# A new opening for a fused state-space and MLP kernel: loads, decay differences and weight decoding in another order

## The chip, the cores and the metric

The kernel runs on one core of a Trainium2 chip. The time is the device time of one execution in microseconds (us). Of the kernel before, three executions were timed: 346.02 us is the median, 344.71 and 346.83 the ends. One more execution was profiled; it took 345.45 us, and the profile's rows are from it. The engines are named as the profile has them: PE (TensorE, matmuls), DVE (VectorE), ACT (ScalarE), POOL (GpSimd) and SP, whose queue issues most transfers. Each engine works through its own instructions in order and waits for others by semaphores.

## What is computed

Two blocks follow each other. The first is a chunked state-space scan (4 batches, 8 heads, 768 positions, head dimension 32, state size 16):

```python
cum = np.cumsum(np.log(a_chunk), axis=-1)
L = np.exp(cum[:, :, :, None] - cum[:, :, None, :]) * causal
M = np.einsum('bhin,bhjn->bhij', Cc, Bc) * L
y = M @ xc + np.einsum('bhin,bhnd->bhid', Cc, state) * np.exp(cum)[..., None]
state = decay_full * state + np.sum(Bx * decay_from_j, axis=2)
```

The second is an MLP on the 3072 tokens of 256 channels that come out of it: `h = x @ w_in` (256x2048), `g = h * clip(h + 3, 0, 6) / 6`, `out = g @ w_out` (2048x256). The weights arrive as float64.

## The kernel before

The 768 positions are cut into six chunks of 128 (c = 0 to 5). A chunk holds the tokens of all four batches (512 columns) and is treated as two halves of 64 positions. Chunk c goes through the scan while TensorE works on the MLP of chunk k = c - 1; only chunk 0 has its scan ahead of everything. The order of all instructions is written out by hand: the calls in the source are the program, and on each engine the instructions stand in the order of the calls. No planner moves them.

**The scan of a chunk.** L, the decay factors, is the exponential of differences of `cum`. For chunks 0 and 1 the differences are made on TensorE: `in_three` splits `cum` into three bf16 parts (`split`), then into a PSUM bank for each batch go a mask (`diff_mask`, L352), a product that subtracts the column's value (`diff_less`, L364) and 16 small products that add the row's (`diff_pick`, L373); `diff_exp` (L381, ACT) takes the exponential. `turn_b` and `turn_squares` turn B and C. `ends` (L412, POOL) scales B by the decay to the end of the half. `scores` makes the products of C and B (`cb`, L543) and, through `into_state` (L555), those of B and x for the state of both halves. `multiply` puts L on the scores in four products on DVE (L585), one for each pair of heads; `mid` (L580) is the state between the halves. `mix` (L611) multiplies with x, for heads 0 to 3 (`ys[..., 0]`) and then 4 to 7, and adds what comes from `mid` (`from_state`, L516). `keep` (L625) copies chunk 0's result to `yT`, and `renew` makes the state for the next chunk.

**The weights.** w_in and w_out arrive in eight blocks of 1 MB (`raw`, three buffers): blocks 0 to 3 are w_in, each four of the 16 column groups f; blocks 4 to 7 are w_out. `decode` takes the 64-bit floats apart and makes float32: exponent and sign on ACT and DVE, the significand on DVE (L209, L213), the sign put back by L236, and a last product (L249) that writes `first_in[i]` or a quarter of `w_out`. It is a generator of five steps; `weights(i, n)` takes n of them. Its fourth step also issues the load of block i + 3 (`load_w`).

**The first MLP pass** (k = 0) is float32. For each f, `mlp_in` makes two products of 512 columns (L636, each issued as two matmuls); `ramp` (L715, ACT) and `times_ramp` (L720, DVE) make g in `gT`. PSUM has four banks for it (`f0` to `f3`, f modulo 4). Between the groups stand the steps of blocks 2 to 5, laid out by the table `weave`: block i has its five steps after f = 4i - 8 to 4i - 4. Then `first_out` (L735) multiplies with w_out, in four quarters that need blocks 4 to 7 in turn, with the scan of chunk 1 and the split of w_in into fp32r parts between them. The later passes use those parts (`lead`, `follow`, L684) and `wide_units` (L861), with the next chunk's scan in fixed places.

**The opening's queues.** On SP: `a`, C in eight pieces, x, block 1, the stores of `cum`, blocks 2 and 3. On ACT's queue: block 0, then B. `busy` is a product whose result nobody reads, called twice.

## Time and profile before

| what | us |
|---|---|
| median of three executions | 346.02 |
| the profiled execution | 345.45 |
| its span, first to last instruction | 343.7 |
| PE busy in the span | 334.6 (97%) |
| DVE / ACT / POOL busy | 220.1 / 173.2 / 142.7 |
| first matmul of the first MLP pass issued | 22.98 |
| first matmul with w_out issued | 50.55 |

A row of the timeline gives the start in us from the start of the span, the duration (of a merged group: from its first start to its last end), the engine, the line, the operation, what it writes and reads, shape and type, and how many were merged; in brackets the idle time of the engine just before and what ended it. Instructions of one engine overlap a little, so the next can start before the last one's duration is over. "PE" rows are matmuls, "PEld" rows the weight loads beside them. `raw` stands in the profile for the weight blocks, `wse` and `wm` for their parts, `w` for the decoded blocks.

### The profile page before, as it was taken

The numbers are of one execution on the slowest core, as the hardware profiler recorded it, in microseconds if no ns is written. First come the engines' busy times: TensorE is split into PE (matmuls) and PEld (weight loads), VectorE is DVE, ScalarE is ACT, GpSimd is POOL, SyncE is SP. The second block draws the span as 40 slices with busy tenths as digits, with TensorE's granted clock in tenths as the row PEclk, the third lists the DMA queues.
The fourth block names the chain that finished last, engine by engine and source line by source line (L and its number), as shares of the span: only waits on it lengthen the run. The fifth ranks groups of instructions, "written<-read, shape, count | busy, mean of one in ns | idle before, by whom it ended". The sixth has DMA issues, their size and how long they took to land.

```text
span 343.7 us, 8181 instructions
## 1 busy us (share of the span) xinstructions
PE 334.6 (97%) x3378; PEld 266.5 (78%) x3378; DVE 220.1 (64%) x357; ACT 173.2 (50%) x359; POOL 142.7 (42%) x139
## 2 busy tenths in 40 slices
PE   6889999999999999999999999999999999999996
PEld 2554448888778888888888888888887788888995
DVE  6689999999698647775438666447666324676011
ACT  4769878738874561564551564561564010565000
POOL 3300000093299923099611199610099400089500
PEclk9999999999999999999999999999999999999999
DMA  8888959206941057242029242051200010200010
GB/s 173 163 341 169 242 187 176 53 2 95 192 61 23 5 69 159 34 60 51 2 34 176 46 56 58 6 64 17 34 13 0 2 19 1 34 12 2 0 33 31
DMA packets 91605, 24.89 MB, mean 72 GB/s; under 512 B 84208, under 2 KB 87952, under 8 KB 91056
## 3 DMA queue, kind: packets, MB, share of 16 engines
q1 hardware_dynamic: 87184, 23.06, 34.8%
q10 hardware_dynamic: 4384, 1.31, 1.7%
q8 instruction: 26, 0.43, 0.5%
q14 instruction: 11, 0.09, 0.1%
HBM read 21.07 MB, written 3.29 MB: 71 GB/s over the span
## 4 chain that ended last, share of the span: by engine, by line
PE 75%; issue 11%; DMA 4%; DVE 2%; ACT 2%; POOL 2%; SPq 2%; POOLq 0%; DVEq 0%
PE h L684 31%; PE wb L861 13%; PE wc L861 8%; PE wa L861 8%; PE oa L794 4%; PE ob L794 4%; PE y L611 2%; PE y L516 2%; DMA raw<-in_moe_w_in_dram 2%; PE cb L543 2%; DMA eto<-cum_e 1%; ACT L L401 1%; POOL bs L412 1%; DMA pairs<-in_C_dram 1%; SPq L321 1%
## 5 line engine op out<-in xcount | busy, mean ns | idle before, releaser
L708 DVE SCALAR_TENSOR_TENSOR gT<-gT,h 128x512 f32<-128x512 f32 x80 | 54.9, 687 | 30.7 <-ACT gT L707 27.9
L707 ACT ACTIVATE gT<-h,half_up 128x512 f32<-128x512 f32 x80 | 55.1, 690 | 33.2 <-PE h L684 33.1
L780 POOL TENSOR_TENSOR s<-gT 128x512 f32<-128x512 f32 x20 | 25.8, 1288 | 66.4 <-DVE gT L708 66.4
L684 PE MATMUL h<-gap,w_gap 128*128 128x512 f32 x160 | 51.8, 409 | 0.0
L684 PE MATMUL h<-high,w_high 128*128 128x512 f32 x160 | 50.7, 398 | 0.1
L684 PE MATMUL h<-low,w_low 128*128 128x512 f32 x160 | 50.3, 395 | 0.0
L700 ACT ACTIVATE h<-h 128x512 f32<-128x512 f32 x40 | 23.5, 588 | 30.4 <-PE h L684 30.4
L684 PEld LDWEIGHTS h<-high,w_high 128*128 128x128 f32 x160 | 29.5, 188 | 8.5 <-DVE h L697 2.1
L684 PEld LDWEIGHTS h<-low,w_low 128*128 128x128 f32 x160 | 30.1, 188 | 7.2
L684 PEld LDWEIGHTS h<-gap,w_gap 128*128 128x128 f32 x160 | 29.9, 188 | 7.1 <-DVE gap L678 0.5
L401 ACT ACTIVATE L<-L,cum_n 128x64 f32<-128x64 f32 x128 | 31.6, 337 | 0.7 <-POOL L L162 0.7
L861 PE MATMUL wb<-s,w_out 128*128 128x256 f32 x128 | 30.7, 382 | 0.0
L419 POOL TENSOR_TENSOR tmp<-state,eto 128x256 f32<-128x256 f32 x5 | 3.6, 721 | 61.0 <-ACT eto L405 60.9
L735 PE MATMUL o<-w_out,gT 128*128 128x256 f32 x128 | 28.7, 381 | 0.0
L697 DVE TENSOR_SCALAR h<-h 128x512 f32<-128x512 f32 x40 | 27.7, 692 | 1.2 <-PE h L684 1.2
L636 PE MATMUL h<-yT,w 128*128 128x512 f32 x64 | 27.7, 594 | 0.0
L780 POOL TENSOR_TENSOR s<-s,gT 128x512 f32<-128x512 f32 x20 | 26.9, 1345 | 1.6
L585 DVE TENSOR_TENSOR L<-L,cb 128x512 f32<-128x512 f32 x24 | 15.3, 682 | 19.1 <-PE cb L543 16.3
L735 PEld LDWEIGHTS o<-w_out,gT 128*128 128x128 f32 x128 | 24.1, 190 | 3.8 <-issue 0.5
L861 PEld LDWEIGHTS wb<-s,w_out 128*128 128x128 f32 x128 | 24.0, 190 | 3.6
L412 POOL TENSOR_TENSOR bs<-B,L 128x128 f32<-128x128 f32 x24 | 13.7, 584 | 30.9 <-ACT L L401 25.8
L780 POOL TENSOR_TENSOR gT<-gT 128x512 f32<-128x512 f32 x20 | 25.9, 1294 | 0.0
(141 smaller groups left out, 534.3 us busy)
## 6 DMA issues: line engine op xcount, KB each, us to landing
raw<-in_moe_w_out_dram SPq DMA_DIRECT2D x4, 1024.0 KB
L<-cum_d SPq DMA_DIRECT2D x8, 512.0 KB
xt<-in_x_dram SPq DMA_DIRECT2D x6, 512.0 KB
raw<-in_moe_w_in_dram SPq DMA_DIRECT2D x3, 1024.0 KB
out_dram<-back SPq DMA_DIRECT2D x128, 16.0 KB
eto<-cum_e SPq DMA_DIRECT2D x20, 64.0 KB
B<-in_B_dram SPq DMA_DIRECT2D x5, 256.0 KB
raw<-in_moe_w_in_dram ACTq DMA_DIRECT2D x1, 1024.0 KB
```

Source lines behind the costliest of these rows:

```text
L401: nc.scalar.activation(Ls[c][:, b, h], Ls[c][:, b, h], AF.Exp, bias=cum_n[:, c, g:g + 1])
L412: nc.gpsimd.tensor_tensor(out=bss[c][:, hs], in0=Bs[c][:, hs], in1=Ls[c][:, b, :, HT - 1:HT].to_broadcast([P, NH, N]), op=ALU.mult)
L636: nc.tensor.matmul(out=h.rearrange("p r i -> p (r i)"), lhsT=first_in[f // FP][:, j, f % FP * P:(f % FP + 1) * P], rhs=yTs[k][:, j], start ...
L684: nc.tensor.matmul(out=h, lhsT=w[:, j, f * P:(f + 1) * P], rhs=y[:, j], start=(start and j == 0), stop=True, skip_group_check=True)
L697: nc.vector.tensor_scalar(out=h, in0=h, scalar1=-Z / UP, scalar2=None, op0=ALU.mult)
L700: nc.scalar.mul(h, h, -Z / UP)
L707: nc.scalar.activation(g, h, AF.Relu, bias=half_up, scale=UP * UP / 6.0)
L708: nc.vector.scalar_tensor_tensor(out=g, in0=g, scalar=UP, in1=h, op0=ALU.min, op1=ALU.mult)
L735: nc.tensor.matmul(out=o[:, b % 2], lhsT=gTs[0][:, f, b * P:(b + 1) * P], rhs=w_out[:, f], start=(f == 0 and b % 2 == 0), stop=True, skip_ ...
L780: nc.gpsimd.tensor_tensor(out=o, in0=p_, in1=q_, op=op)
L794: nc.tensor.matmul(out=bank[:, slot], lhsT=lhs[:, j], rhs=rhs[:, j], start=(clear and j == 0), stop=True, skip_group_check=True)
L861: nc.tensor.matmul(out=bank[:, slot], lhsT=lhs[:, j], rhs=rhs[:, j], start=(clear and j == 0), stop=True, skip_group_check=True)
```

## The change

- **Loads.** C of chunk 0 now comes in one transfer with tokens first, on ACT's queue; B follows `a` on SP. Block 0 is loaded in two halves of 512 KB. The first follows B, the second and blocks 1 and 2 are held: `hold` writes one word of the buffer on GpSimd, with an operand that some earlier step produces, and the load has to wait for that write. The second half waits for the first step of `fade_end`, block 1 for the end of `multiply(0)`, block 2 for the second half of `yT`.
- **Decay differences.** `spread_heads` writes `split` eight times over, once for each head with all other heads zeroed: for chunk 0 half on DVE and half on ACT, for chunk 1 on POOL. `diff_rows` then adds the row's value with two products of 512 columns for each batch in place of `diff_pick`'s 16. Chunk 1's batch 3 is done after f = 1 of the first MLP pass; its exponentials after f = 4, 5, 7.
- **C of chunk 0** is turned on TensorE (`turn_c`, bank `y1`); `fade_end` makes the faded second half on POOL out of the two parts.
- **State.** For chunk 0, `into_state` is called for each half by itself: the first half's after the scores, the second's behind the mixing; `take` and `renew(0)` come later, the latter after f = 13.
- **Decoding.** The exponent comes from `Abs` on ACT; the two `and` steps on DVE go, and the sign is put back by one SCALAR_TENSOR_TENSOR, in blocks 6 and 7 by a product with `Sign` from ACT. Blocks 0 and 1 are decoded in halves (`decode_half`): block 0 around the mixing, block 1 after f = 1 and 2. `weave` starts three groups later, and `by_token` moves to ACT. Both calls of `busy` go.
- **Later chunks.** `apart`, with which the two halves of a mix are issued in different units, holds for chunk 4 too.

```diff
-        Bs[c] = tokens_first(B, nc.scalar if c == 0 else nc.sync, name="B")
-        if c == 0:
-            bcs[c] = [pairs_first(C), Bs[c]]
-        elif c < TURN:
+        if c < TURN:
+            bcs[c] = [tokens_first(C, nc.sync if c else nc.scalar, name="C", tag="bc")]
+        Bs[c] = tokens_first(B, name="B")
...
+    def hold(t, after):
+
+        nc.gpsimd.tensor_copy(t.bitcast(FP32), after)
...
+        signed = i >= NP + 2
+        nc.scalar.activation(e.bitcast(BF16), top.bitcast(BF16), AF.Abs)
...
-        nc.vector.tensor_scalar(
-            out=e, in0=s, scalar1=0x7FF0, scalar2=None, op0=ALU.bitwise_and)
-        nc.vector.tensor_scalar(
-            out=s, in0=s, scalar1=0x8000, scalar2=None, op0=ALU.bitwise_and)
...
+        if signed:
+            nc.vector.tensor_tensor(out=e, in0=e, in1=s, op=ALU.mult)
+        else:
+            nc.vector.scalar_tensor_tensor(
+                out=e.bitcast(U16), in0=top, scalar=0x8000, in1=e.bitcast(U16),
+                op0=ALU.bitwise_and, op1=ALU.bitwise_or)
+        if i + NRAW < 2 * NP:
+            load_w(i + NRAW)
+        yield
         nc.vector.scalar_tensor_tensor(
             out=dst, in0=m, scalar=unit, in1=e, op0=ALU.mult, op1=ALU.mult)
...
+    def diff_rows(c, b):
+        for a, rows in enumerate(HALF):
+            nc.tensor.matmul(
+                out=ds[c, b][rows], lhsT=by_batch[:, b:b + 1].to_broadcast([P, HT]),
+                rhs=spread[c][:, :, rows], start=False, stop=True,
+                tile_position=(0, a * HT), skip_group_check=True)
...
+    for b in range(3):
+        mask(0, b)
+    spread_heads(0, nc.vector, range(NH // 2))
+    spread_heads(0, nc.scalar, range(NH // 2, NH))
+    spread_heads(1, nc.gpsimd, range(NH))
+    add_up(ends_at[1])
+    for b in range(NB):
+        diff_less(0, b)
+    for b in range(2):
+        diff_rows(0, b)
+    turn_c(0, turn_ps(0, 0))
+    for b in range(2, NB):
+        diff_rows(0, b)
     for b in range(NB):
         diff_exp(0, b)
+    turn_b(0)
     first_eto()
...
+    part_early(0)
+    halves = [decode_half(0, u) for u in range(2)]
+    next(halves[0])
+    next(halves[0])
+    fading = fade_end(0)
+    load_half(1, next(fading)[0:1, 0, 0:1])
+    next(fading)
     scores(0)
+    for b in range(2):
+        diff_less(1, b)
+    for b in range(2):
+        diff_rows(1, b)
+    into_state(0, 0)
     multiply(0)
+    load_w(1, Ls[0][0:1, 0, NH - 1, 0:1])
+    next(halves[0])
+    yTs[0] = y_tile("yT", FP32)
+    mix(0, (0,))
+    keep(0, 0)
+    mix(0, (1,))
+    into_state(0, 1)
+    keep(0, 1)
+    c_ps = ps.tile([P, NC, G], FP32, name="c_ps", tag="f3")
+    turn_cum(c_ps)
+    take(0)
+    load_w(2, yTs[0][0:1, 1, 0:1])
+    for _ in range(3):
+        next(halves[1])
+    by_token(c_ps)
     load_w(3)
...
     for i in range(2, NP + 2):
         for j in range(5):
-            weave.setdefault(4 * i - 8 + j, []).append(i)
-    weave[NF - 1].append(NP + 2)
+            weave.setdefault(4 * i - 5 + j, []).append(i)
...
                 for i in weave.get(f, []):
                     weights(i, 1)
-                if f in (6, 8):
-                    diff_exp(c, f // 2 - 3)
+                if f in (1, 2):
+                    for _ in range(3):
+                        next(halves[f - 1])
+                if f == 1:
+                    diff_mask(c, 3)
+                    diff_less(c, 3)
+                    diff_rows(c, 3)
+                elif f == 2:
+                    load_w(1 + NRAW)
+                elif f == 13:
+                    renew(0)
+                if f in (4, 5, 7):
+                    diff_exp(c, {4: 3, 5: 0, 7: 1}[f])
...
-                apart = c in (TURN, NC - 1)
+                apart = c >= TURN
```

## The prediction

> **What bounds the kernel now.** I read the profile's slices first. TensorE (PE) is in the nines from the third slice of 8.6 us to the end, VectorE (DVE) only until about 86 us.

> ```profile
> ## 2 busy tenths in 40 slices
> PE   6889999999999999999999999999999999999996
> ...
> DVE  6689999999698647775438666447666324676011
> ```

> Then the table by stretches, cut where the stages change (columns: stretch, its length, each engine's busy time, clock, DMA). The first product of the first MLP pass is issued at 22.98 and the first product with w_out at 50.55.

> ```profile
> 0.00:23.00 23.00, 17.38 (x451) 10.07 (x451) 17.12 (x37) 12.75 (x22) 5.80 (x18) 1.00 0.90 226
> 23.00:50.50 27.50, 27.50 (x66) 12.24 (x65) 24.92 (x39) 23.40 (x30) 0.00 (x0) 1.00 0.84 195
> 50.50:66.00 15.50, 15.50 (x73) 13.61 (x72) 15.12 (x21) 12.20 (x12) 0.00 (x0) 1.00 0.86 153
> 66.00:85.00 19.00, 18.95 (x391) 15.94 (x389) 17.47 (x25) 11.61 (x36) 12.52 (x12) 1.00 0.26 42
> ```

> From 23 us on, TensorE never waits (27.50 of 27.50, 15.50 of 15.50; the table of waits for it is empty from 50 us to the end). So the time is the moment when the first MLP product starts, plus TensorE's work, plus every wait put into that work. VectorE is nearly as full: 24.92 of 27.50, since between the ramps of the first pass it also decodes the weights. The third view is the timeline of VectorE in that pass:

> ```profile
> 34.06 1.23 DVE L249 SCALAR_TENSOR_TENSOR w<-wm,wse 128x1024 f32<-128x1024 f32 x1
> 35.21 0.68 DVE L720 SCALAR_TENSOR_TENSOR gT<-gT,h 128x512 f32<-128x512 f32 x1
> ...
> 37.20 0.68 DVE L720 SCALAR_TENSOR_TENSOR gT<-gT,h 128x512 f32<-128x512 f32 x1
> 38.50 0.69 DVE L720 SCALAR_TENSOR_TENSOR gT<-gT,h 128x512 f32<-128x512 f32 x1 [0.62 <-ACT gT L715]
> 39.11 1.22 DVE L213 SCALAR_TENSOR_TENSOR wm<-raw,wm 128x1024 f32<-128x1024 uint32 x1
> 40.25 0.68 DVE L720 SCALAR_TENSOR_TENSOR gT<-gT,h 128x512 f32<-128x512 f32 x1
> 40.84 0.68 DVE L236 TENSOR_TENSOR wse<-wse 128x1024 uint16<-128x1024 uint16 x1
> 41.56 1.23 DVE L249 SCALAR_TENSOR_TENSOR w<-wm,wse 128x1024 f32<-128x1024 f32 x1
> ```

> L249 is the last step of a weight block. Block 2 (columns f = 8 to 11) is finished at 35.29; its first product is due at 22.98 + 8 x 1.72 = 36.74 (four matmuls of 0.43 for each f). Block 3 is finished at 42.79 and due at 43.62, block 4 (w_out) at 49.8 and due at 50.55. Each is ready only about one column early, and that because its last step stands behind the ramp of f = 4, 8, 12, three columns ahead of its use.

> **The change: the start of the MLP.** In both kernels the decay sums are split at 7.50 (7.08 + 0.42). From there, with rows of before:
> - Spreading: four ScalarE instructions of 128x128. L401 (128x64) takes 0.34 and starts every 0.25; with 64 more elements about 0.3 each, 1.3 in all, to 8.85. VectorE's half (128x512 in bf16, between 0.2 and 0.68) ends earlier. GpSimd's part for chunk 1 (128x1024) lies between 2 x 1.01 (L271, 128x512) and 2 x 1.35 (L780): about 2.6, beside all this.
> - Row products: two 512-column matmuls for each batch instead of 16 small ones, 0.25 and about 0.2 until ScalarE sees them: 9.3. The four Exp take 2.25 (8.57 to 10.82 in before): 11.55. B's copy (0.59) and the eto Exp (0.39): 12.6.
> - C is needed at 9.4 now, B at 10.5. In before C's last piece came at 12.6, issued behind 1 MB of weights. C and B of chunk 1, issued from 27.7 to 32.5, moved at 52 to 167 GB/s; 0.6 MB with `a` then lie by about 8 us. x (released at 15.99 in before) follows half a weight block, not a whole one: about 12.
> - Scores 1.3 (14.86 to 16.12): 13.9. The four products of multiply 2.48: 16.4, against 18.60. This is 2.2 us earlier.
> - Mixing's first half runs under multiply now; one `busy` product (1.12) and the second half of the state no longer stand ahead. What follows multiply is the other half (21.58 to 22.98: 1.40), 32 state products (half of L555's 0.86) and turn_cum (0.36): the first MLP product at 18.6 instead of 22.98. **-4.4.**

> ScalarE's half decode (3 x about 0.7) fits between its Exp of chunk 1 and `mid`, and VectorE's two steps on it between cT and multiply. If POOL's spread took 4 us, its four bs (1.53) would end at 13.1, still ahead of multiply.

> **In the first pass.** mask, less and two row products of (1, 3) now stand after f = 1: 3 x about 0.22. **+0.65.** The weave moves from 4i-8 to 4i-5, so that the last step of block i is recorded after f = 4i-1: behind the ramp product of the very column before the one that needs it. VectorE works in order. The chain from the end of column 7 to the start of column 8 is then serial: ramp on ScalarE begins 0.29 after TensorE's last issue (28.14 to 28.43 at f = 2) and takes 0.67; VectorE follows after 0.03; L720 holds it 0.61 (38.50 to 39.11); the last step 1.22; 0.06 to the matmul. That is **2.9 us in which TensorE has nothing else**, where before it had no wait. The same stands at f = 12 and, with block 4's last step after f = 15, ahead of the first w_out product.

> At f = 8 VectorE is late besides. From 16.4 it has the rest of block 0 (1.2 + 2.0), block 1 in halves after f = 1 and 2 (4.1), eight L720 (4.9), block 2 (0.61 + 1.14 + 1.14 + 1.22): 16.3 us of work, and 2.6 of waiting for ScalarE, which does adds and three decode steps before it lets block 0's second half go, and about 1.8 in smaller waits. That ends at 37.2; TensorE is there at 18.6 + 0.65 + 13.76 = 33.0. **+4.2** instead of 2.9. At f = 12 the wait has refilled everything: **+2.9.** Before the first w_out product, renew (0.42 + 0.61, moved to f = 13) makes VectorE a us late again: **+3.9.** I laid all the steps of the pass end to end, engine by engine, for before too: it gives 35.1, 42.9 and 50.5 for block 2, block 3 and the first w_out product, where the trace has 35.29, 42.79 and 50.55.

> The sign step is now one SCALAR_TENSOR_TENSOR of 128x1024 on 16 bits, which before doesn't show: between L236's 0.68 and L249's 1.23. I take 1.22, since L213 and L249 both have it; at 0.68 the waits sum to 10.0, not 11.0. The two dropped `and` steps (0.42 + 0.43 a block) and by_token (0.28) are taken off VectorE, included above.

> The held loads: raw1 is issued after multiply, 16.6; raw0 in before took 5.95 from issue (0.80) to use (6.75), so 22.6, needed at 22.9. A us later would put a us on the sum, the high side of my range. raw2 is issued near 18.9, needed at 27.7: covered. On SP only loads for later stand behind the held ones.

> **Later.** `apart` now takes in chunk 4. By the chain of waits the passes from wa to wa or oa take 51.55 and 51.57 with an undivided mix (chunks 2 and 4), 51.93 with a divided one (chunk 3): **+0.35.** From the first w_out product on, TensorE's order and work are the same; between 50.55 and 107.98 it idles about 1 us, so nothing is left to absorb a late start.

> **Sum**: -4.4 + 0.65 + 4.2 + 2.9 + 3.9 + 0.35 = +7.6 on the profiled execution's 345.45 (span 343.7): 353.1. That execution lies 0.57 under the median of 346.02, so the median comes to **353.5**.

> **Rivals.**
> - *The clock falls in the waits.* The eight mask matmuls from 2.14 to 5.50 start every 0.43; later ones of the same shape (7.56 to 8.09 for two) every 0.26. So TensorE runs at half rate at the start, for the 3.8 us until 5.9. If a wait near 4 us brings that back, 1.9 us is lost each time, at f = 8 and before w_out: 355.4 to 357.3. Against it: no gap after 23 us in before shows it either way. 0.13. [...]
> - *The start doesn't move.* A late x, C or spread keeps the first product at 21 to 22; the waits come all the same: 356 to 357. For it: 0.6 MB in 64-byte rows ahead of everything. Against it: more than a us of cover at each. 0.08.
> - *Faster: VectorE's stream is what ends the section, and the waits are given back.* VectorE has about 3.5 us less decode work and a start 2.2 earlier. If TensorE's waits sum to under 3.4, the early start wins: with none, 342.0. It decides at that point. But three serial chains of 2.9 come to 8.7 with VectorE never late, and TensorE has no idle time later to return them. 0.03; partly so, within 1%: 0.05.

> The forecast has 0.71. A measurement can tell about 1% from no change, so faster by over 1% (under 342.6) 0.03, within 1% 0.06, slower 0.91. The range: the sum with the quicker sign step and a start at 17 is 350.4, less a us for what else may run quicker; raw1 a us late and the clock falling twice reach 358.3. I take 349.5 to 358.3.

> **What would show it.** The first MLP product at 17.5 to 20; TensorE's waits on VectorE ahead of f = 8, f = 12 and the first w_out product of 3.5 to 4.5, 2.9 and 3 to 4 us; the first w_out product near 58; bodies after it as long as before. Wrong if those waits are under 1 us each, or the first product comes after 21.

## The result, and the profile after

The changed kernel takes 359.27 us (median of four executions, 357.84 to 364.41) against 345.61 of the kernel before (median of four, three of them the ones named at the start): 1.038 times as long, with a 95% interval of 1.032 to 1.044 (the execution of 364.41 had a lower clock, 0.971, and is left out of the ratio). The forecast was 353.5 and its range ended at 358.3. Slower was right; the size was 5.8 us short. The profiled execution took 360.05, its span is 358.3.

The slices of the page, and then the table by stretches (columns as before), cut at the first MLP product and at the first product with w_out:

```profile
## 2 busy tenths in 40 slices
PE   6997776999999999999999999999999999999996
...
DVE  7968358797878764767443867345776323577011
...
PEclk9999689899999999999999999999999999999999
```

```profile
0.00:18.50 18.50, 14.97 (x336) 8.34 (x336) 15.84 (x34) 11.70 (x26) 10.13 (x23) 1.00 1.10 139
18.50:63.10 44.60, 34.16 (x70) 13.75 (x68) 29.41 (x42) 30.21 (x42) 0.00 (x0) 0.89 0.67 168
63.10:80.00 16.90, 16.86 (x70) 14.60 (x71) 14.13 (x15) 11.87 (x12) 0.00 (x0) 0.90 1.02 168
```

The opening is shorter, 18.50 in place of 22.98. The first pass is longer, 44.60 in place of 27.57, and TensorE is idle for 10.4 of it. New is the value behind POOL's, the granted clock: 0.89 in the first pass and 0.90 in the stretch behind it, where the kernel before had 1.00 in every stretch. The timeline of TensorE in the first pass has the waits:

```profile
18.50 3.70 PE L704 MATMUL h<-yT,w 128*128 128x512 f32 x8
...
22.89 10.74 PE L704 MATMUL h<-yT,w 128*128 128x512 f32 x24
37.70 10.19 PE L704 MATMUL h<-yT,w 128*128 128x512 f32 x16 [4.07 <-DVE w L261]
50.56 8.83 PE L704 MATMUL h<-yT,w 128*128 128x512 f32 x16 [2.67 <-DVE w L261]
63.13 17.46 PE L803 MATMUL o<-w_out,gT 128*128 128x256 f32 x72 [3.75 <-DVE w_out L261]
```

f = 8 to 11 and f = 12 to 15 are 16 matmuls each of the same shape. At full clock such a group takes 7.13 (measured below); here they took 10.19 and 8.83. The trace's record of the granted clock has three stretches at half speed after the start: 37.06 to 43.89, 50.72 to 54.13 and 64.37 to 67.78. The products lose half of the time in which they run there, 37.70 to 43.89 and the other two stretches whole: 3.1 + 1.7 + 1.7 = **6.5 us**. The groups' durations say the same: 10.19 and 8.83 are 3.06 and 1.70 over 7.13, and the 72 w_out products of 17.46 took 15.81 at full clock (the spread steps, below), 1.65 less.

With that the 14.6 us between the two spans are accounted for: -4.48 (start), +0.86 (the products for chunk 1's batch 3, 22.03 to 22.89), +10.49 (three waits), +0.8 (0.27 for each wait: it is counted from the end of the last matmul, 0.16 after the next could have started, and behind it the second matmul starts 0.10 later than the others do), +6.5 (clock), +0.3 (`apart`), which is 14.5.

### The profile page after: what moved, and what is told of

It is laid out like the page before. It is cut to its first block, busy times and chain, and to the rows that moved or that the text cites. A ratio compares the mean times of both kernels' runs of the same rounds, so it can differ in the third digit from the quotient of the medians.

```text
span 358.3 us, 7973 instructions
## 1 busy us (share of the span) xinstructions
PE 340.9 (95%) x3267; PEld 267.4 (75%) x3267; DVE 220.1 (61%) x350; ACT 178.3 (50%) x373; POOL 145.2 (41%) x144
## 4 chain that ended last, share of the span: by engine, by line
PE 86%; ACT 6%; DVE 5%; DMA 1%; issue 1%; ACTq 0%
PE h L752 30%; PE wb L929 12%; PE o L803 8%; PE wc L929 8%; PE wa L929 8%; PE h L704 4%; PE oa L862 3%; PE ob L862 3%; PE y L681 2%; PE y L585 2%; PE cb L612 2%; ACT gT L783 2%; PE y L625 1%; DVE gT L788 1%; DVE wse L255 1%; DMA pre<-in_a_dram 1%
## 5 line engine op out<-in xcount | busy, mean ns | idle before, releaser
L776 DVE SCALAR_TENSOR_TENSOR gT<-gT,h 128x512 f32<-128x512 f32 x80 | 54.9, 687 | 30.8 <-ACT gT L775 28.0
L848 POOL TENSOR_TENSOR s<-gT 128x512 f32<-128x512 f32 x20 | 25.7, 1287 | 63.5 <-DVE gT L776 32.2
L704 PE MATMUL h<-yT,w 128*128 128x512 f32 x64 | 33.5, 682 | 6.7 <-DVE w L261 6.7
L803 PE MATMUL o<-w_out,gT 128*128 128x256 f32 x128 | 30.4, 397 | 3.7 <-DVE w_out L261 3.7
L704 PEld LDWEIGHTS h<-yT,w 128*128 128x128 f32 x64 | 13.5, 217 | 25.4 <-issue 15.0
L467 ACT ACTIVATE L<-L,cum_n 128x64 f32<-128x64 f32 x128 | 31.6, 337 | 0.0
L803 PEld LDWEIGHTS o<-w_out,gT 128*128 128x128 f32 x128 | 25.2, 199 | 8.3 <-ACT wse L234 4.5
L929 PE MATMUL wb<-s,w_out 128*128 128x256 f32 x128 | 30.6, 382 | 0.0
L765 DVE TENSOR_SCALAR h<-h 128x512 f32<-128x512 f32 x40 | 27.7, 691 | 1.2 <-PE h L752 1.2
L848 POOL TENSOR_TENSOR s<-s,gT 128x512 f32<-128x512 f32 x20 | 26.9, 1346 | 1.6
L175 POOL TENSOR_SCALAR_AFFINE_SELECT L<-L 64x1024 f32<-64x1024 f32 (+1 forms) x16 | 20.9, 1312 | 15.6 <-DMA L<-cum_d 15.2
L655 DVE TENSOR_TENSOR L<-L,cb 128x512 f32<-128x512 f32 x24 | 15.3, 681 | 18.8 <-PE cb L612 16.0
L929 PEld LDWEIGHTS wb<-s,w_out 128*128 128x128 f32 x128 | 24.0, 190 | 3.6
```

The source lines that it names most:

```text
L175: nc.gpsimd.affine_select(out=t[rows], in_=t[rows], pattern=pattern, compare_op=ALU.is_ge, fill=-1e5, base=base, channel_multiplier=-1)
L467: nc.scalar.activation(Ls[c][:, b, h], Ls[c][:, b, h], AF.Exp, bias=cum_n[:, c, g:g + 1])
L704: nc.tensor.matmul(out=h.rearrange("p r i -> p (r i)"), lhsT=first_in[f // FP][:, j, f % FP * P:(f % FP + 1) * P], rhs=yTs[k][:, j], start ...
L765: nc.vector.tensor_scalar(out=h, in0=h, scalar1=-Z / UP, scalar2=None, op0=ALU.mult)
L776: nc.vector.scalar_tensor_tensor(out=g, in0=g, scalar=UP, in1=h, op0=ALU.min, op1=ALU.mult)
L803: nc.tensor.matmul(out=o[:, b % 2], lhsT=gTs[0][:, f, b * P:(b + 1) * P], rhs=w_out[:, f], start=(f == 0 and b % 2 == 0), stop=True, skip_ ...
```

## Which part makes the waits

The theory is the prediction's: the weave puts the last step of a block behind the ramp product of the column just ahead of its use. Its rival: the waits come from the new opening, from late loads or from the halves of blocks 0 and 1. The kernel before, with the new weave alone:

```diff
-            weave.setdefault(4 * i - 8 + j, []).append(i)
-    weave[NF - 1].append(NP + 2)
+            weave.setdefault(4 * i - 5 + j, []).append(i)
...
-            weights(NP + 1, 1)
+            weights(NP + 1, 4)
+            weights(NP + 2, 1)
```

> The kernel before with one edit: the steps of blocks 2 to 5 start three groups later (4i-5 for 4i-8), as in the changed kernel. Theory: the last step of a block behind the ramp of the column before its use makes TensorE wait by itself; from the rows of before, 3.9 us at f = 8, 3.5 at f = 12, 3.5 ahead of w_out, and the clock falls as in the changed kernel (5 to 7 us): 361 to 364. Rival: the waits come from the new opening (held loads, block 1 decoded in the pass): then 345 to 348.

It is 1.040 times as long as the kernel before (1.033 to 1.047). The profiled execution took 358.40, less than the 361 to 364 expected, since the clock fell only once in it, for 3.41 us. Its timeline of TensorE:

```profile
40.58 8.83 PE L636 MATMUL h<-yT,w 128*128 128x512 f32 x16 [3.75 <-DVE w L249]
52.79 7.13 PE L636 MATMUL h<-yT,w 128*128 128x512 f32 x16 [3.38 <-DVE w L249]
63.39 6.93 PE L735 MATMUL o<-w_out,gT 128*128 128x256 f32 x31 [3.47 <-DVE w_out L249]
```

The same three waits stand there with the old opening and the old decoding. So the weave's shift of three columns is enough for them; nothing of the new opening is needed. The loads were tested by themselves, in the changed kernel without the three `hold` writes:

```diff
-        nc.gpsimd.tensor_copy(t.bitcast(FP32), after)
+        pass
```

> The changed kernel without the three writes of GpSimd: the second half of block 0 and blocks 1 and 2 are loaded as soon as their queue comes to them. By the prediction the holds bring nothing on the path, since TensorE is busy from the state products on and the first half of block 0 stands ahead: the first MLP product stays at 18.5 (within 0.3), the waits of the pass at 4.1, 2.7 and 3.8, and the time at 357 to 361. If the holds keep the opening's small loads free, x, B or block 0 land later and the start goes to 19.5 or beyond.

The start is at 18.71, the waits are 4.07, 2.67 and 3.74, the time of the one execution 355.83. That is under the expected 357 to 361 because the clock fell for one window of 3.41 us and not for four. Holding the loads does nothing for the start or the waits. One column less of delay, in the changed kernel (`4 * i - 6`):

> The changed kernel with the steps of blocks 2 to 5 one group earlier, so that the last product of block 2 (L261) stands ahead of the ramp product of f = 7 on DVE and no longer behind it; everything else as in the changed kernel. If the three waits are the queue on DVE (the last step behind the ramp products), they shrink to about 3.1, 1.2 and 2.2 us, worked out by replaying the rows' durations; the first w_out product comes near 53.3 plus what the clock takes (up to 1.7 us for each stretch of 3.41 at half speed), and the time is 350 to 351.5 us without a fall, up to 354 with two. If the waits came from somewhere else (the weights' loads, ACT's steps), they stay at 4.1, 2.7 and 3.8 and the time at 358 to 360.

The waits fell to 2.73, 0.94 and 2.03, close to the replayed 3.1, 1.2 and 2.2:

```profile
42.25 8.83 PE L704 MATMUL h<-yT,w 128*128 128x512 f32 x16 [2.73 <-DVE w L261]
52.01 7.13 PE L704 MATMUL h<-yT,w 128*128 128x512 f32 x16 [0.94 <-DVE w L261]
```

The ratio is 1.015 (1.012 to 1.018), and two of the four executions took 350.73 and 350.98. In the profiled one, 356.63, the opening lost 2.55 us in the mix on a wait that has no releaser in the profile (more on it at the end), with half clock behind it (18.78 to 25.61). The queue on DVE, and how far ahead of its use a step stands in it, sets these waits.

## Is the rest the clock?

The remaining 6.5 us were read off one execution. If the clock falls because TensorE stands still, products that nobody reads, put into the waits, keep it up and leave the waits' own length. Two kernels: such products ahead of f = 8, f = 12 and the first w_out product, 4, 3 and 4 of them, and half as many (2, 1, 2).

```diff
+                if f in (8, 12):
+                    busy({8: 4, 12: 3}[f])
                 mlp_in(k, f)
...
+            busy(4)
```

> The changed kernel with products that nobody reads (0.86 us each) put into TensorE's three waits of the first MLP pass: 4 ahead of f = 8, 3 ahead of f = 12, 4 ahead of the first w_out product, so that 0.6, 0.1 and 0.3 us of each wait stay idle. Theory: the three waits cost 10.5 us by themselves and 6.9 us more because TensorE runs at half clock after each. Then the clock stays at 1.0 and the time is 352.4 (351.5 to 353.5). Rival: the products after the waits are slow for another reason (memory traffic, VectorE); then nothing moves, 358 to 360.

> The same with 2, 1 and 2 products, so that idle stretches of about 2.3, 1.8 and 2.0 us are left. If only a stretch of 2.5 us or more brings the clock down, the clock stays up and the time is that of the filled kernel, 352.4. If a stretch of 2 us is enough, 356 to 360.

The timeline of TensorE with the waits filled:

```profile
44.48 7.13 PE L712 MATMUL h<-yT,w 128*128 128x512 f32 x16 [0.63 <-DVE w L261]
...
54.28 7.13 PE L712 MATMUL h<-yT,w 128*128 128x512 f32 x16
...
65.16 7.14 PE L811 MATMUL o<-w_out,gT 128*128 128x256 f32 x32 [0.31 <-DVE w_out L261]
```

Both groups take 7.13, and the clock is full from 28.03 to the end. What it lost came earlier: a wait of 2.36 us in the opening's mix, again without a releaser, and half clock from 17.79 to 28.03, so that the MLP started at 22.60. Its executions took 356.22 to 362.63 (ratio 1.037, 1.027 to 1.048), all above the expected 352.4. That was a little low: the changed kernel's 360.05 less 6.5 is 353.55. The profiled execution also has two more waits without a releaser, 1.29 at 96.30 and 0.29 at 143.15. The best one, at full clock throughout, was not profiled: why it took 356.22 is not known. Half filled, the waits were 2.37, 1.81 and 2.03, the ratio 1.028 (1.021 to 1.034). The two executions at full clock took 353.62 and 354.23, which is the 353.55; the profiled one, which fell once (38.70 to 42.11), took 355.83, the fourth 358.43. That is neither of the two outcomes expected: with idle stretches of about 2 us (1.81 to 2.37 in the profiled one) the clock fell in two executions (0.995 and 0.989 over the whole) and not in the two others (1.000).

Now the three kernels can be set side by side. From the first MLP product to the first w_out product, less half of what ran at half clock: changed kernel 63.13 - 18.50 - 4.80 = 39.83; filled 65.16 - 22.60 - 2.72 = 39.84; half filled 60.18 - 18.59 - 1.71 = 39.88. The way from one to the other is the same whether TensorE idles in the waits or not, and all that differs is the clock. The 6.5 belong to the profiled execution of the changed kernel, whose clock was 0.980 over the whole; those of 357.84 and 358.5, with 0.985 and 0.984, lie 4.3 and 5.0 above the 353.55. The prediction's sum has 39.2 for this distance (57.8 - 18.6).

**When does it fall?** In all executions that were profiled, every change of the clock lies a whole multiple of 3.413 us from the others of that execution; where this grid begins differs from execution to execution. So I cut the pass of the changed kernel along that grid (columns as before: the first pair behind the length is TensorE's busy time, the value behind POOL's is the clock):

```profile
33.65:37.06 3.41, 0.00 (x0) 0.00 (x0) 3.13 (x5) 2.48 (x4) 0.00 (x0) 1.00 1.57 139
37.06:40.47 3.41, 2.77 (x4) 1.22 (x5) 0.59 (x1) 0.00 (x0) 0.00 (x0) 0.50 0.90 270
40.47:43.89 3.42, 3.42 (x6) 1.35 (x5) 1.29 (x2) 1.72 (x2) 0.00 (x0) 0.50 0.93 358
47.31:50.72 3.41, 0.74 (x3) 0.16 (x2) 3.20 (x4) 1.70 (x2) 0.00 (x0) 1.00 0.12 30
50.72:54.13 3.41, 3.41 (x5) 1.35 (x6) 0.00 (x0) 0.00 (x0) 0.00 (x0) 0.50 0.72 277
57.54:60.95 3.41, 1.85 (x5) 0.54 (x3) 3.38 (x6) 2.38 (x4) 0.00 (x0) 1.00 0.00 0
60.95:64.37 3.42, 1.24 (x6) 1.14 (x7) 3.39 (x5) 3.35 (x4) 0.00 (x0) 1.00 0.48 144
64.37:67.78 3.41, 3.41 (x10) 2.70 (x9) 3.38 (x4) 0.63 (x2) 0.00 (x0) 0.50 1.33 236
```

A grid window in which TensorE was busy for 0.00, 0.74 or 1.24 us is followed by one at half clock; one with 1.85 is not. Half clock ends here after a window that was busy throughout (40.47 to 43.89), not after one busy for 2.77. Over the seventeen profiled executions, between 14 and 112 us, of the windows at full clock: all eleven that were idle for 64% or more were followed by half clock; of eight idle for 51 to 58%, three; of those idle for less, one, in the opening's mix of small 64x64 products (42%). What decides among the eight is open. So in these runs it is not the length of a wait that counts but how much of one window it takes up: the wait of 2.67 us lay in one window and cost 1.7 us, while in the half-filled kernel those of 1.81 and 2.03 lay across an edge (at most 1.45 in one window) and cost nothing. Nor did the longer wait of 3.38 in the kernel before with the late weave, which an edge cut into 1.89 and 1.48:

```profile
47.89:51.30 3.41, 1.52 (x4) 0.38 (x2) 2.85 (x4) 3.25 (x4) 0.00 (x0) 1.00 0.00 0
51.30:54.72 3.41, 1.93 (x5) 0.97 (x6) 1.40 (x2) 0.00 (x0) 0.00 (x0) 1.00 0.85 278
```

## Can the early start be kept?

If the weave is the whole loss, the changed opening with the steps spread so that each block is ready in time should be faster than the kernel before. In the changed kernel:

```diff
-    for i in range(2, NP + 2):
-        for j in range(5):
-            weave.setdefault(4 * i - 5 + j, []).append(i)
+    for i, places in ((2, (2, 2, 2, 2, 3)), (3, (4, 5, 6, 6, 8)), (4, (8, 9, 11, 11, 12)), (5, (15,))):
+        for f in places:
+            weave.setdefault(f, []).append(i)
```

with block 4's load ahead of the steps, the loads for chunk 1 (eto, bc, x) after f = 3, `renew(0)` behind the pass, and the exponentials after f = 4, 8, 11.

> The changed kernel with the steps of blocks 2, 3 and 4 in other places: four steps of block 2 after f = 2 and its last after 3; block 3 after 4, 5, 6, 6, 8; block 4 after 8, 9, 11, 11, 12; the load of block 4 and block 2's step ahead of the loads of chunk 1 on SP; renew(0) after the pass; exponentials after 4, 8, 11. Theory: the early start (18.5) is worth its 4.5 us once no last step stands right ahead of its use; by the rows, one wait of 1.1 us is left, the first w_out product comes near 48 and the time is 343.4 (342 to 345). Rival: VectorE and ScalarE have too much to do for an early start, wherever the steps stand: 346 to 350.

347.38 us, 1.004 times the time before (1.002 to 1.006), where 342 to 345 was expected. The pass now has one wait of 1.24, and the first w_out product comes 1.8 us earlier than in the kernel before. Then the gain is lost:

```profile
48.73 15.81 PE L803 MATMUL o<-w_out,gT 128*128 128x256 f32 x72
...
72.54 0.61 PE L585 MATMUL y<-csT,state 32*64 32x64 f32 x25 [1.94 <-DVE csT L531]
```

DVE has chunk 1's faded C behind four fp32r splits; half clock from 73.50 to 76.92 follows. I took these waits one by one. Each edit keeps the ones ahead of it unless it says otherwise.

Faded C two splits earlier, block 2's splits later (`gap_w(2)` behind the multiply, `low_w(2)` after f = 5 of the second pass):

> The kernel of the spread steps, with chunk 1's faded C (csT, L531) two of the fp32r splits earlier on DVE: before the pair of block 1 instead of behind it, and the pair of block 2 later. In the spread-steps run TensorE waited 1.94 us for it at 72.5 and then ran 3.41 us at half clock, which together took the 1.8 us gained before it and more. If that wait is where the gain went, the wait and the half-clock stretch go: 345.7 - 1.9 - 1.5 gives a span near 342.3 and a time of 343.9 to 344.6 us, 0.2 to 0.5% under the kernel before. If something else holds the section (the scan's multiply, the store of the results), another wait takes its place and the time stays at 346.5 to 347.4.

1.006 (1.003 to 1.009). The wait for csT is gone, and three came in its place: 0.83 for L746 at 82.9, 0.61 for L726 and 1.13 for L765 around 100, with half clock from 101.08. Beside it ran the same kernel with the change to `apart` undone:

```diff
-                apart = c >= TURN
+                apart = c in (TURN, NC - 1)
```

> The same kernel with the change to later chunks undone: `apart` holds for TURN and the last chunk alone, as before. The prediction set the extra unit for chunk 4 at 0.35 us, from the difference of chunks 3 and 5; by that this run is 0.3 to 0.4 us under the run beside it (343.5 to 344.2). If the split of the mix gives something back, it is the same or slower.

1.014 (1.010 to 1.017), slower than the kernel beside it. In its profile the undivided mix has a wait of 1.23 us without a releaser (231.35) and takes 3.58 us to the next product instead of 2.04 in the kernel before. From the last stage of the second pass (first L929, L861 in the kernel before) to the end it took 237.26; less those 1.54, 235.72, as the kernel before (235.75), while with the divided mix it is 236.07. Some 0.3 of the prediction's 0.35 (taken there from chunk 3 against 2 and 4) are there, but undoing them gave nothing in time.

On the first of these two: the fourth step of block 2 after f = 3, and the splits of block 2 in halves in the second pass, ahead of block 3's:

> The kernel with the faded C early, with DVE's work laid out once more: the fourth step of block 2 after f = 3 and no longer after f = 2 (the wait of 1.23 us ahead of f = 7, for the ramp product of f = 3), and the fp32r split of block 2 in halves between the groups of the second pass, ahead of block 3's (the waits of 0.83, 0.61 and 1.13 us in that run for L746, L726 and L765). If these waits are what was left of DVE's queue, the first w_out product comes at 47.5 to 47.9, the four waits shrink to under 0.3 each, and the span falls from the 345.6 of its undisturbed runs by 2.5 to 3.8: 341.8 to 343.1, a time of 343.5 to 344.8 us and 0.2 to 0.6% under the kernel before. If DVE has no room for the opening's gain at all, other waits of the same size show up by f = 16 of the second pass, and the time stays at 346 to 347.5.

1.007 (1.004 to 1.010). Waits of 0.53 and 1.01 in the first pass, 0.82 and 0.92 later: other waits of the same size. From the spread steps again, with `renew(0)` and chunk 2's second decay moved and the faded C early:

> The kernel of the spread steps with three moves in the section of chunk 1's scan, each against a wait that was seen there: `renew(0)` goes to the place where DVE stood idle for 2.66 us (57.4 to 60.07), the faded C ahead of the fp32r splits of blocks 1 and 2, which keep their place before the multiply, and the decay of chunk 2's second batch behind the mix, so that ACT (L467 until 79.3) is free when the mix ends near 78.0. If the gain was lost to these three queues, the first w_out product stays at 48.7, the wait of 1.94 us and the one for L746 are under 0.3, the second pass's last stage (first L929) begins at 106.2 to 106.6 in place of 109.62, and with 236.05 from there to the end the span is 342.2 to 342.7, the time 343.9 to 344.4 us, 0.3 to 0.4% under the kernel before. If another engine paces the section in any case (GpSimd's masks for the decay, L175), the time is 345.5 to 347.

1.002 (1.001 to 1.003), 346.11 to 346.33 in eleven executions. Besides the 1.24 in the first pass, left were 0.75 for the second w_out block, put off by `renew(0)`, and 0.87 for L746.

> The kernel before this one in the row (the scan section laid out anew) with two corrections: `renew(0)` one decoding step earlier, so that it lies in DVE's idle time of 2.65 us ahead of L253 and no longer behind it (it put off the second w_out block, a wait of 0.75 us), and the first sum of the w_out parts (L830) behind the products for the split of y (a wait of 0.87 us for L746), with the third one in the second pass. By DVE's queue both waits fall under 0.3 us, the second pass's last stage begins at 106.7 to 107.2 in place of 108.37, the span is 342.8 to 343.3 and the time 344.4 to 345.0 us, 0.1 to 0.3% under the kernel before. If ACT's or GpSimd's part of the section paces it, the time stays at 345.8 to 346.3.

This is the best of the series: 0.997 times the time before, with an interval of 0.994 to 1.000, which does not tell it from no change. Besides the 1.24, its wait is now in the mix, and DVE's timeline shows why:

```profile
70.31 1.43 DVE L731 SCALAR_TENSOR_TENSOR w_gap<-w_high,w 128x1024 fp32r<-128x1024 f32 x1
71.67 2.16 DVE L726 SCALAR_TENSOR_TENSOR w_low<-w_high,w 128x1024 fp32r<-128x1024 f32 x1
73.75 2.16 DVE L731 SCALAR_TENSOR_TENSOR w_gap<-w_high,w 128x1024 fp32r<-128x1024 f32 x1
75.84 1.27 DVE L655 TENSOR_TENSOR L<-L,cb 128x512 f32<-128x512 f32 x2
```

The splits take 1.22 at 65.36 and 2.16 here, where GpSimd has its masks (L175, 70.62 to 78.13). The mix waits 1.09 and 0.19 behind them. The last three runs moved one split out from there, into the second pass: its halves after f = 3 and 5; after f = 1 and 3; and then the third sum of w_out's parts after f = 12 in place of f = 5.

> The last kernel with the split `gap_w` of block 2 (L731, 2.16 us at 73.75 beside GpSimd's masks) taken out from ahead of chunk 1's multiply and done in two halves after f = 3 and f = 5 of the second pass. If DVE's queue ahead of the multiply is what is left, the waits of 1.09 and 0.19 us of the mix go, the halves cost 0.69 each in idle time of DVE, and the time is 1.0 to 1.3 us under the last run's: 343.6 to 344.8 us, 0.2 to 0.5% under the kernel before. If GpSimd's masks pace the section, the wait comes back for L655, L740 or L765 and the time stays at 344.9 to 345.9.

> The last kernel with the two halves of the split after f = 1 and f = 3 of the second pass in place of f = 3 and f = 5, and the third sum after f = 5. The wait of 3.83 us, and the 6.83 us at half clock that came before its end, came from the half that stood behind the ramp product of f = 5; with two groups of room they go, and the gain at 82.65 (1.6 us before the kernel before) is kept: the second pass's last stage begins at 106.2 to 106.7, the span is 342.2 to 342.8, the time 343.4 to 344.5 us, 0.3 to 0.6% under the kernel before. If DVE has no room for the halves there either, a wait of 0.5 us or more shows up in the second pass and the time stays at 345 or above.

> The last kernel with the third sum of the w_out parts (L830) after f = 12 of the second pass in place of f = 5. In the last run it took 2.23 us at 95.58 beside GpSimd's sums, and the product behind it (L765) came 1.97 us late for TensorE. If that one operation is what is left, the wait goes: the undisturbed runs of the last kernel had a span of 345.1, less 2.0 gives 343.1, a time of 344.3 to 345.0 us, 0.1 to 0.3% under the kernel before. If the stretch is full with what else DVE does there (the halves at 1.0 to 1.2 us in place of 0.69), a wait of 0.5 us or more comes back between f = 6 and f = 14 and the time stays at 345.5 or above.

1.014, 1.004 (1.002 to 1.007) and 1.003 (1.001 to 1.004). In all three the waits of the mix went and the last w_out product of the pass stood near 82.7, 1.6 us ahead of the kernel before. The first of them then repeats the change's own mistake in small:

```profile
97.33 0.79 PE L752 MATMUL h<-gap,w_gap 128*128 128x512 f32 x1 [3.83 <-DVE w_gap L731]
```

The half stood behind the ramp product of f = 5 (L776) for a product that TensorE issues right behind f = 5. In the other two TensorE waits 1.97 (at 100.16) and 1.54 (at 107.74) for L765. A row of the second of the three from DVE: the sum that takes 1.22 elsewhere,

```profile
95.58 2.23 DVE L830 TENSOR_TENSOR t<-w_out,t 128x1024 f32<-128x1024 f32 x1
```

beside GpSimd's sums (L848). So in every order tried, what TensorE gained turned into waits for DVE further on, and no version here beats the kernel before. From 66 to 86 us DVE has little room: it was busy for 18.7 to 19.8 of the 20 us in the first six versions, for 17.3 in the last three. From 86 to 108 us, where the last waits stand, it was busy for 16.9 to 20.0 of 22, so there the order and single slow operations make the waits. Whether another order keeps the gain is not shown.

## What slows DVE in the opening

In the changed kernel the prefix sum of 512 columns took 2.91 us, 1.21 in the kernel before. This run has it behind `turn_c`, so that it no longer starts together with GpSimd's product for chunk 1's heads:

```diff
     spread_heads(1, nc.gpsimd, range(NH))
-    add_up(ends_at[1])
...
     turn_c(0, turn_ps(0, 0))
+    add_up(ends_at[1])
```

> The changed kernel with the prefix sum of the later 512 columns (L335) behind the turning of C on DVE, so that it no longer runs beside GpSimd's product for chunk 1's heads. If the two engines slow each other, the sum takes 1.2 to 1.5 us in place of 2.91, the two products of `turn_c` stand at 9.4 to 10.8 in place of 10.26 to 11.63, and the GpSimd product takes less than its 2.39; if the 2.91 belong to the operation at this place, they stay. The start stays at 18.3 to 18.5 in either case, since the exponentials and `first_eto` on ACT (until 11.64) hold the scores, and the time at 356 to 361.

DVE in the kernel before, in the changed kernel, and in this one:

```profile
14.63 1.21 DVE L282 TENSOR_TENSOR_SCAN pre<-pre 32x512 f32<-32x512 f32 x1
```

```profile
7.42 2.91 DVE L335 TENSOR_TENSOR_SCAN pre<-pre 32x512 f32<-32x512 f32 x1
10.26 1.37 DVE L525 TENSOR_SCALAR cT<-t_ps,parity 128x512 f32<-128x512 f32 x2
```

```profile
9.61 1.41 DVE L525 TENSOR_SCALAR cT<-t_ps,parity 128x512 f32<-128x512 f32 x2 [1.94 <-PE t_ps L506]
10.93 1.20 DVE L335 TENSOR_TENSOR_SCAN pre<-pre 32x512 f32<-32x512 f32 x1
```

1.20 in place of 2.91, and C is turned 0.65 earlier. GpSimd's product took 2.39 both times, so there it is DVE that gives way. It is not always DVE: in its new place the sum (10.93 to 12.13) runs beside one of GpSimd's products for B (L478), which started later, at 11.11, and took 1.24, where the three ahead of it took 0.41 or 0.42. Each time the operation that started later ended last: in the changed kernel the sum at 10.33, 1.1 after GpSimd's product was over, and here GpSimd's product at 12.35, 0.2 after the sum. The start (18.68, expected 18.3 to 18.5), the waits and the time (358.23) stayed, so the slow sum cost the changed kernel nothing.

## Why the prediction was wrong in size, step by step

- **The start, -4.4: right** (18.50 for 18.6; -4.48). Part of this is luck, since two errors cancel. Multiply ended at 15.65, not 16.4, since `split` was ready at 6.78, not 7.50; and from there to the first MLP product it took 2.85, not 2.2. TensorE's own work behind the scores sets the end, without a wait over 0.2 from 14.07 on, and the prediction had the chain through multiply set it. The end of TensorE's row:

```profile
16.15 0.86 PE L681 MATMUL y<-L,xt 64*32 64x64 f32 x64
16.94 0.68 PE L585 MATMUL y<-csT,mid 32*64 32x64 f32 x16
17.55 0.65 PE L625 MATMUL y<-xt,bs 64*32 64x64 f32 x32
18.14 0.43 PE L400 MATMUL c_ps<-ident,pre 32*128 32x32 f32 x4
```

- **The inserted products, +0.65:** 0.86.
- **The waits, +4.2, +2.9, +3.9: right in place, cause and size.** The profile counts 4.07, 2.67 and 3.75 from the last matmul's end; from where the next could have started, as the prediction counts, they are 0.16 longer: 4.2, 2.8 and 3.9. The chain is the predicted one; the second value is DVE's duration:

```profile
34.70 1.22 DVE L255 SCALAR_TENSOR_TENSOR wse<-raw,wse 128x1024 uint16<-128x1024 uint16 x1
35.83 0.68 DVE L788 SCALAR_TENSOR_TENSOR gT<-gT,h 128x512 f32<-128x512 f32 x1
36.43 1.22 DVE L261 SCALAR_TENSOR_TENSOR w<-wm,wse 128x1024 f32<-128x1024 f32 x1
```

L255 is the sign step that the trace before did not show: 1.22, the value taken.
- **The held loads, cover or a us late:** cover; without the holds neither the start nor a wait moves by more than 0.2.
- **`apart`, +0.35:** 0.3, from the distance to the end.
- **The step that failed is the clock's term in the sum: put at 0, and measured at 6.5 us.** Without it the changed kernel is at 353.55, and the forecast was 353.5. The prediction knew the fall as a rival, with 0.13, and priced it at 1.9 us in two places. It happened in three, and once over two windows, for 3.1, 1.7 and 1.7. Two assumptions failed. "Against it: no gap after 23 us in before shows it either way" was taken for evidence against, where it was no evidence. And the fall was tied to "a wait near 4 us", so that the wait of 2.67 counted as safe, where a window idle for 64% was enough (eleven of eleven). The rival's 355.4 to 357.3 were also too low by the third fall and the second window.
- **The other rivals** did not come true. The start moved. "VectorE's stream is what ends the section" is true of DVE behind the first pass, but against the change: with the waits out of the pass, the waits for DVE take the early start back by the second pass's end. The prediction, with TensorE full from 50 us on, had not looked there.
- **Three small slips** change nothing: 353.1 and 0.57 make 353.7, not 353.5; the 342.0 of the last rival is on the profiled execution, on the median it is 342.6; and between 50.55 and 107.98 TensorE idles 0.13 us in the kernel before, not about 1.

## What to carry to other kernels

A step that another engine waits for must not stand behind the result of the work just ahead of its use: here DVE's last step of a block stood in its queue behind the ramp product, which made the chain serial and its length a wait each time round, 4.07, 2.67 and 3.75 us. When a change adds waits to a TensorE that had none, price the clock with them: here a window of 3.41 us that was idle for 64% or more was followed by half clock each time (eleven of eleven), at 1.7 us for a window of full work, and one idle for 51 to 58% in three cases of eight. And the early start, 4.48 us here, was worth only what DVE's queue gave room for in the orders tried: look at the next engine's idle time, and at the order of its queue, as far as the first place where the gain could wait.
